# Seven half products instead of eight for the gate matmuls of the last two token chunks, and a written order for the kernel's tail

## The chip, the cores and the metric

The kernel runs on one core of one Trainium2 chip. The metric is the device time of one execution in microseconds (us), lower is better. In the text PE is the matmul engine (TensorE), PEld its weight loads, DVE the VectorE, ACT the ScalarE, POOL the GpSimd and SP the engine whose queue issues the output DMAs. PSUM is the matmul accumulator memory, eight banks of 512 fp32 values per partition.

## The reference

An attention stage feeds a gated feed-forward layer. Only the second is touched by the change.

```python
# 8 batches x 8 heads x 576 positions x 64: pooled (4:1) attention plus banded local attention
attn_out = out_up + out_local
x = attn_out.transpose(0, 2, 1, 3).reshape(4608, 512)
# feed-forward, d_model 512, d_ff 1536
gate = np.maximum(x @ w_gate, 0.0)
val  = x @ w_val
out  = gate * val @ w_out            # 4608 x 512, float32
```

## The kernel before

Heads are worked in 32 pairs. For each pair the kernel loads q, k and v, transposes q and k, computes scores, exponentials and their products with v, and writes the normalised result, transposed, into `xT` (128 partitions x 4 blocks of the model dimension x 4608 tokens, fp16). The feed-forward layer runs over nine chunks of 512 tokens (`TCH`), c = 0 to 8, and over twelve blocks of 128 columns of d_ff, jj = 0 to 11. Attention of later pairs and feed-forward of earlier chunks are interleaved.

The first layer for one chunk and one block (`emit_h_mm`, line 588) is four matmuls of 128x128 by 128x512 with `wg_sb` into one PSUM bank (the gate part) and four with `wv_sb` into the next bank (the value part). ACT then writes `relu` of the gate bank to an fp16 tile (`emit_relu`, L605), and DVE multiplies that by the value bank into `gT` (`emit_gate`, L609). `gT` has two buffers, one for even and one for odd chunks.

The second layer is already done in seven products. A `Unit` (chunk c, half u of 256 tokens) splits the product of `gT` and `wo_sb` into 2 x 2 blocks: 128 tokens, 768 of d_ff, 256 output columns. DVE makes the sums `s1` to `s4` of blocks of `gT` (`sums`, L678); those of the weights, `wt`, were made once. The products `p1` to `p7` are six 256-column matmuls each (`mm`, L684). They accumulate in three PSUM regions `a`, `b` and `d`: ACT copies `a` out after p1, p6 and p7 (`keep`, L718), DVE adds a copy to `d` or `b` (`c11` L721, `c12` L725, `c22` L733), ACT copies the last `a` (`c21` L729), and SP issues the output DMAs (L635).

The order on all engines is written by the kernel: within each engine, instructions run as they were emitted, and the framework only adds the semaphore waits. Chunks 2 to 6 run from a token list (`ORDER`, by `emit_periods`). The tokens with `<` belong to the chunk before: the last two gate multiplications of chunk 6 (`gate/5`, `gate/4`) and the first sums of its second unit (`next/0`, `next/1`) are emitted at the head of the following period.

The rest, the tail, is emitted by loops. `emit_tail_slot` takes three blocks jj of chunks 7 and 8 at a time. It puts one product of a unit of the chunk before between two blocks, and defers each block's relu and gate multiplication until the next block's matmuls have been emitted. Chunk 7 or 8 uses banks 0 to 3 (pairs 0 and 1) for the first layer, and the unit in work uses one bank for each of its regions (4, 5 and 6). At the end the two units of chunk 8 run interleaved, the first in banks 4, 5 and 6, the second in 7, 2 and 3:

```python
        for p in ("p2", "p6", "p5", "p7", "p4", "p3"):
            for x in last:
                x.step(p)
```

POOL has no work after the attention stage: its row is empty in the last 11 of 40 slices of the span.

Of the kernel before, what the change touches and what calls it, by code (L numbers as in the profile page):

```python
# [83 lines left out]
def kernel(  # L84
# [28 lines left out]
    NK = NJJ // 2  # L113
# [5 lines left out]
    keep = ctx.enter_context(tc.tile_pool(name="keep", bufs=1))  # L119
# [22 lines left out]
    qkfull = ring(NL, [128, 2, 2 * NB * 64], FP16, "qk16_")  # L142
# [4 lines left out]
    vwfull = ring(NL, [128, 2 * NB, 128], FP16, "vw_")  # L147
# [14 lines left out]
    gT = ring(2, [128, NJJ, TCH], FP16, "gT_")  # L162
    xT = keep.tile([128, NPB, NTOK], FP16, name="xT")
    ps = psum.tile([128, 8, 512], FP32, name="ps")
# [8 lines left out]
    sa = [  # L173
        [vwfull[r].rearrange("p b c -> p (b c)")[:, 768 * i : 768 * (i + 1)]
         .rearrange("p (j t) -> p j t", t=128) for r in rs for i in range(2)]
        for rs in ((4, 5), (6, 0))
    ]
# [25 lines left out]
    def pair(i):  # L203
        return ps[:, 2 * i : 2 * i + 2, :]
# [377 lines left out]
        else:  # L582
            nc.vector.tensor_copy(out=o, in_=pair(pp)[:, :, 0:288])

    def emit_h_mm(c, jj, pp, which, kks):
        w = (wg_sb, wv_sb)[which]
        for kk in kks:
            nc.tensor.matmul(  # L588
                out=pair(pp)[:, which, :],
                lhsT=w[:, kk, bass.ts(jj, 128)],  # L590
                rhs=xT[:, kk, c * TCH : (c + 1) * TCH],
                start=(kk == 0),
                stop=(kk == 3),
            )

    def emit_h(c, jj, pp, parts=((0, range(4)), (1, range(4))), relu=False):
        for which, kks in parts:
            emit_h_mm(c, jj, pp, which, kks)

        r = emit_relu(pp) if relu else None  # L600
        return lambda: emit_gate(c, jj, pp, emit_relu(pp) if r is None else r)

    def emit_relu(pp):
        r1 = ffn.tile([128, TCH], FP16, name="r1", tag="r1")
        nc.scalar.activation(out=r1, in_=pair(pp)[:, 0, :], func=AF.Relu)  # L605
        return r1

    def emit_gate(c, jj, pp, r1):
        nc.vector.tensor_tensor(  # L609
            out=gT[c % 2][:, jj, :], in0=r1, in1=pair(pp)[:, 1, :], op=ALU.mult  # L610
        )

    def emit_y(c, ty, bank, cut=0, inner=None):
# [39 lines left out]
    units = {}  # L653

    class Unit:


        def __init__(self, c, u, regions, ss, ms, split):
            self.c, self.u, self.split, self.done = c, u, split, []
            self.a, self.b, self.d = (ps[:, k, lo : lo + 256] for k, lo in regions)  # L660
            self.s1, self.s2, self.s3, self.s4 = ss
            self.m1, self.m2, self.m3 = ms
            g = gT[c % 2]
            self.x = [
                [g[:, NK * i : NK * (i + 1), 256 * u + 128 * t : 256 * u + 128 * t + 128] for i in range(2)]
                for t in range(2)
            ]
# [49 lines left out]
        def keep(self, i):  # L717
            nc.scalar.copy(out=(self.m1, self.m2, self.m3)[i], in_=self.a)  # L718
# [29 lines left out]
        def out(self, t, k):  # L748
            if self.split:
                emit_out(self.c, 2 * self.u + t, self.y[t], nc.sync, 256 * k, 256 * k + 256)  # L750
            else:
                self.done.append(t)
                if self.done.count(t) == 2:
                    emit_out(self.c, 2 * self.u + t, self.y[t], nc.sync)
# [51 lines left out]
        emit_s2(hp, 6, 0)  # L806
        emit_warm(1)

    def tail_unit(c, u, banks=(4, 5, 6)):
        return Unit(c, u, [(k, 0) for k in banks], sa[u], sums[u], True)  # L810

    def slot_unit(s):

        c, u = s // 4 - 1, s % 4 // 2
        if s >= NP - LEAD:
            return tail_unit(c, u)
        k = 2 * (((s - PS) // 2 + 1) % 2)
        return Unit(c, u, ((k, 0), (k + 1, 0), (k + 1, 256)), sx, sums[0], False)

    def emit_tail_slot(s, gate):  # L820
        c, jj = s // 4, 3 * (s % 4)
        gate()
        if s % 2 == 0:
            if s == NP - LEAD:
                w = units[s]
                w.sums(5, NK, range(2))
                w.step("p1")
                w.sums(which=range(2, 4))
                emit_h_mm(c, jj, 1, 0, range(3))
                emit_h_mm(c, jj, 1, 1, range(3))  # L830
                w.step("p2")
                emit_h(c, jj, 1, ((0, range(3, 4)), (1, range(3, 4))))()
                emit_h(c, jj + 1, 0)()
            else:
                w = units[s] = slot_unit(s)
                w.sums()
                w.step("p1")
                emit_h(c, jj, 0)()
                w.step("p2")
                emit_h(c, jj + 1, 1)()  # L840
            w.step("p6")
            w.step("p5")
        else:
            w = units[s - 1]
            w.step("p7")
            emit_h(c, jj, 0)()
            w.step("p4")
            if s == 4 * NCH - 1:
                last[0].sums(0, 4)
            emit_h(c, jj + 1, 1)()  # L850
            w.step("p3")
            if s == 4 * NCH - 1:
                last[1].sums(0, 4)
        return emit_h(c, jj + 2, 1 if s == NP - LEAD else 0)

    def unit(c, u):
        s = 4 * (c + 1) + 2 * u
        if s not in units:
            units[s] = slot_unit(s)
        return units[s]  # L860

    relus = {}

    def emit_step(kind, arg, u, c):

        banks = (u, 1 - u)
        i = int(arg[-1]) if arg and arg[-1].isdigit() else 0
        if kind in H_STEPS:
            pp, jj = banks[i % 2], 6 * u + i
            if kind == "relu":  # L870
                relus[c, u, i] = emit_relu(pp)
            elif kind == "gate":
                emit_gate(c, jj, pp, relus.pop((c, u, i)))
            else:
                emit_h_mm(c, jj, pp, int(kind == "hv"), range(4))
        elif kind in UNIT_STEPS:
            UNIT_STEPS[kind](unit(c - 1, u), i)
        elif kind == "next":
# [48 lines left out]
    def emit_periods(c0, c1):  # L927
        for base in range(c0 - 2, c1 + 2):
            for tok in ORDER.split():
                c = base + {">": 1, "<": -1}.get(tok[-1], 0)  # L930
                kind, arg, u = tok.rstrip("<>").split("/")
                if c0 <= c < c1 or c == c0 - 1 and f"{kind}/{arg}/{u}" in LATE:
                    emit_step(kind, arg, int(u), c)

# [71 lines left out]
    with tc.manual_schedule(engines={ET.PE, ET.DVE, ET.Activation, ET.SP, ET.Pool}):  # L1006
        nc.scalar.dma_start(cst_sb[:, 960:1080], cst_dr[:, 960:1080])
        emit_in(0)
        nc.sync.dma_start(cst_sb[:, 0:960], cst_dr[:, 0:960])
        nc.sync.dma_start(cst_sb[:, 1080:1368], cst_dr[:, 1080:1368])  # L1010
        for hp in range(1, 4):
            emit_in(hp)
        emit_warm(10)
        emit_qkT_pe(0, 2, 3)
        emit_pads()
        emit_warm(3)
        for hp in range(LEAD):
            emit_fill(hp)
        gate = None
        for s in range(PS):  # L1020
            gate = emit_slot(s, gate)
        emit_periods(PS // 4, (NP - LEAD) // 4)
        last = [tail_unit(NCH - 1, u, b) for u, b in ((0, (4, 5, 6)), (1, (7, 2, 3)))]
        gate = lambda: None
        for s in range(NP - LEAD, NCH * 4):
            gate = emit_tail_slot(s, gate)
        gate()
        for x in last:
            x.step("p1")
        for which in (range(2), range(2, 4)):  # L1030
            for x in last:
                x.sums(4, NK, which)
        for p in ("p2", "p6", "p5", "p7", "p4", "p3"):
            for x in last:
                x.step(p)


# [28 lines left out]
```

## Time and profile before

| what | before |
|---|---|
| median of 6 runs | 350.24 us (348.64 to 352.86) |
| the profiled execution | 349.6 us |
| its span, first to last instruction | 347.8 us |
| PE busy | 339.5 us (98%) |
| DVE busy | 272.9 us (78%) |
| ACT busy | 214.6 us (62%) |
| POOL busy | 191.0 us (55%) |
| mean granted PE clock | 0.995 of full speed |

The profile's page gives, for each engine, the busy time over the span; then the same in 40 slices; then the DMA queues, the chain of work that ended last, and groups of instructions with the mean duration of one. Further views cut the trace into stretches, or list the instructions of a stretch in order of time. Consecutive instructions of one engine overlap a little, so their starts lie closer together than their durations say; [...]its real pace is read from starts. The tail is the stretch from 274.75 us, where the first product of unit (6, 0) starts, to the end.

### The profile page before, as it was taken

Reading aid. Unit: us, or ns where it says so; the run is one execution under the profiler, and the core shown is the slowest. Engines: PE = TensorE matmul, PEld = TensorE weight load, DVE = VectorE, ACT = ScalarE, POOL = GpSimd, SP = SyncE. Lnnn points to the kernel's source line nnn. Section 1 sums busy time; section 2 is a strip of 40 time slices with the busy share of each in tenths; the row PEclk is TensorE's granted clock in tenths of the full one; section 3 lists DMA queues with packets and bytes.
Section 4 is the critical chain, followed back from the end, with each engine's and each line's share of the span. In section 5 each row is a group of like instructions: output and inputs, shape, how many; then the busy total and the mean of one; then the engine's idle time right before and its main releaser. Section 6 shows DMA issues by size and latency. Waiting matters only on the chain. (4 is left out here: it accounts for less than half of the span.)

```text
span 347.8 us, 7968 instructions
## 1 busy us (share of the span) xinstructions
PE 339.5 (98%) x3127; PEld 205.1 (59%) x3127; DVE 272.9 (78%) x479; ACT 214.6 (62%) x390; POOL 191.0 (55%) x233
## 2 busy tenths in 40 slices
PE   6999999999999999999999999999999999999996
PEld 2665555555565756565666556665666555555575
DVE  4896656788799999999999999999989745354481
ACT  3667777586666776677667767676777443333332
POOL 8985656999999893979398949740300000000000
PEclk9899999999999999999999999999999999999999
DMA  9999999999999999999999998990101001001013
GB/s 144 165 171 186 186 190 164 168 149 192 174 158 147 168 182 83 133 146 188 81 121 166 155 102 103 151 156 10 61 3 60 2 30 47 30 32 45 18 45 121
DMA packets 168772, 40.29 MB, mean 116 GB/s; under 512 B 150080, under 2 KB 165664, under 8 KB 168736
## 3 DMA queue, kind: packets, MB, share of 16 engines
q0 software_dynamic: 132960, 22.93, 88.9%
q1 hardware_dynamic: 35056, 15.79, 24.6%
q10 hardware_dynamic: 720, 1.08, 0.9%
q8 instruction: 24, 0.39, 0.5%
q14 instruction: 12, 0.10, 0.1%
HBM read 46.45 MB, written 9.44 MB: 161 GB/s over the span
## 5 line engine op out<-in xcount | busy, mean ns | idle before, releaser
L588 PE MATMUL ps<-xT,wg_sb 128*128 128x512 f16 x432 | 110.0, 380 | 0.1
L588 PE MATMUL ps<-xT,wv_sb 128*128 128x512 f16 x432 | 109.6, 379 | 0.4 <-DVE gT L609 0.4
L609 DVE TENSOR_TENSOR gT<-r,ps 128x512 f16<-128x512 f16 x108 | 73.0, 682 | 38.1 <-PE ps L588 30.7
L605 ACT ACTIVATE r<-ps 128x512 f16<-128x512 f32 x108 | 64.2, 595 | 49.3 <-PE ps L588 47.6
L588 PEld LDWEIGHTS <-wv_sb 128*128 128x128 f16 x432 | 41.0, 98 | 47.0 <-issue 1.0
L588 PEld LDWEIGHTS <-wg_sb 128*128 128x128 f16 x432 | 39.9, 98 | 36.9 <-DVE xT L581 0.6
L545 DVE TENSOR_TENSOR xn<-ps,rden 64x720 f16<-64x720 f32 x46 | 41.6, 905 | 7.1 <-ACT rden L541 6.2
L376 ACT ACTIVATE ee<-ps 112x576 f16<-112x576 f32 x64 | 38.1, 648 | 10.6 <-PE ps L366 9.5
L536 ACT ACTIVATE rden<-ps 64x720 f32<-64x720 f32 x46 | 35.2, 765 | 14.7 <-PE ps L526 13.7
L233 POOL DMA_DIRECT2D qk<-in_q_dram x46 | 33.7, 735 | 6.9 <-DMA wo_sb<-in_moe_w_out_dram 2.8
L327 POOL TENSOR_TENSOR vd<-v 72x256 f16<-72x256 f32 x23 | 20.4, 896 | 30.6 <-PE ps L526 30.0
L382 DVE TENSOR_TENSOR ee<-ee,cst_sb 112x576 f16<-112x576 f16 x64 | 31.6, 512 | 3.6 <-ACT ee L376 2.6
L684 PEld LDWEIGHTS <-gT 128*128 128x128 f16 x288 | 28.2, 98 | 10.3
L233 POOL DMA_DIRECT2D qk<-in_k_dram x46 | 33.7, 735 | 0.5 <-DMA qk<-in_k_dram 0.4
L258 POOL DMA_DIRECT2D vw<-in_v_dram x30 | 28.7, 957 | 7.5 <-PE ps L294 2.6
L275 DVE TENSOR_REDUCE qkd<-qkT 128x288 f16<-128x1152 f16 x23 | 30.9, 1344 | 0.0
L321 POOL TENSOR_TENSOR v<-v 72x512 f32<-72x512 f16 x23 | 29.0, 1262 | 3.1 <-DMA v<-in_v_dram 2.6
L718 ACT COPY q<-ps 128x256 f32<-128x256 f32 x39 | 14.5, 372 | 20.9 <-PE ps L684 20.7
L684 PEld LDWEIGHTS <-xo 128*128 128x128 f16 x240 | 22.7, 98 | 6.5 <-DVE xo L678 0.8
L684 PE MATMUL ps<-wo_sb,gT 128*128 128x256 f16 x192 | 24.9, 273 | 0.0
L504 DVE TENSOR_TENSOR xT<-xn 128x576 f16<-128x576 f16 x28 | 21.6, 772 | 0.6
L390 ACT ACTIVATE ed<-ps 72x576 f16<-72x576 f32 x32 | 20.6, 643 | 0.0
(103 smaller groups left out, 476.4 us busy)
## 6 DMA issues: line engine op xcount, KB each, us to landing
out_dram<-y_sb SPq DMA_DIRECT2D x20, 256.0 KB, 3.0
vw<-in_v_dram POOLq DMA_DIRECT2D x30, 168.0 KB, 6.8
qk<-in_q_dram POOLq DMA_DIRECT2D x46, 72.0 KB, 6.1
qk<-in_k_dram POOLq DMA_DIRECT2D x46, 72.0 KB, 6.3
v<-in_v_dram POOLq DMA_DIRECT2D x23, 144.0 KB, 6.3
out_dram<-y_sb SPq DMA_DIRECT2D x22, 128.0 KB, 1.7
wg_sb<-in_moe_w_gate_dram POOLq DMA_DIRECT2D x4, 384.0 KB, 9.6
wv_sb<-in_moe_w_val_dram POOLq DMA_DIRECT2D x4, 384.0 KB, 10.8
```

What stands on the lines that cost most here:

```text
L233: nc.gpsimd.dma_start(dst.rearrange("p (j h d) -> p j h d", h=2, d=64)[:, :, hh, :], _dap(src, off + hh * S * D, [[D, 96], [NQ * D, NB], [ ...
L258: nc.gpsimd.dma_start(t, _dap(v, base, [[D, WK], [NQ * D, n], [1, D]]))
L275: nc.vector.tensor_reduce(out=qkd[hp % 2].rearrange("p i t -> p (i t)"), in_=qkT[hp % 4][:, 0 : 2 * S].rearrange("p (t f) -> p t f", f=4), ...
L321: nc.gpsimd.tensor_tensor(out=m, in0=t[:, :, 0:128], in1=t[:, :, 128:256], op=ALU.add)
L376: nc.scalar.activation(out=o, in_=ps[0:WK, p0 + 2 * g : p0 + 2 * g + 2, 0:288], func=AF.Exp, scale=scale)
L382: nc.vector.tensor_tensor(out=o, in0=o, in1=_sap(masks_sb, (0, WK), 288 * g, [[0, 2], [1, 288]]), op=ALU.mult,)
L536: nc.scalar.activation(out=rden[lo : lo + 64], in_=ps[de : de + 64, 4 + 2 * hh : 6 + 2 * hh, 0:360], func=AF.Ln)
L545: nc.vector.tensor_tensor(out=xn[lo : lo + 64], in0=ps[lo : lo + 64, 4 + 2 * hh : 6 + 2 * hh, 0:360], in1=rden[lo : lo + 64], op=ALU.mult,)
L588: nc.tensor.matmul(out=pair(pp)[:, which, :], lhsT=w[:, kk, bass.ts(jj, 128)], rhs=xT[:, kk, c * TCH : (c + 1) * TCH], start=(kk == 0), st ...
L605: nc.scalar.activation(out=r1, in_=pair(pp)[:, 0, :], func=AF.Relu)
L609: nc.vector.tensor_tensor(out=gT[c % 2][:, jj, :], in0=r1, in1=pair(pp)[:, 1, :], op=ALU.mult)
L684: nc.tensor.matmul(out=out, lhsT=left[:, i, :], rhs=right[i], start=(first and i == 0), stop=(i == NK - 1), skip_group_check=True,)
```

## The change

The gate part of chunks 7 and 8 is regrouped into six pairs per chunk of d_ff blocks (j, j + 6), j = 0 to 5. For ten of these twelve pairs (chunk 7 with j = 2 to 5, chunk 8 with j = 0 to 5) the gate part is computed in seven half products; the other two pairs, and the value part of all pairs, stay direct. A pair is a product of 256 columns of d_ff by 512 of the model dimension by 512 tokens, split into 2 x 2 blocks, and a half product `q1` to `q7` is two matmuls of 256 columns.

- DVE makes four sums of the gate weights (`wg`, each 128 x 2 x 768, once) and four sums of `xT` for each of the two chunks (`xs`, each 128 x 2 x 256). They are kept in space that is no longer in use: the q/k tiles and `xT` of chunks 1 and 2.
- A `Block` has three regions in two banks: `a` in bank k, `b` and `d` in the two halves of bank k + 1, with k = 0 for even j and 2 for odd j. ACT copies `a` after q1, q6 and q7 (`keepg`, 128x256 fp32); DVE adds a copy to `d` (`tg/11`), to `b` (`tg/22`, and `tg/12` after q3); ACT copies the last `a` (`tg/21`). The four results lie in SBUF as fp32.
- The relu of these pairs is no longer an ACT instruction: `gateg`, a DVE `scalar_tensor_tensor`, takes max(gate, 0) from SBUF times the value part from PSUM.
- The value part uses bank 4 for block j and bank 5 for block j + 6. The units have regions in two banks, `a` in one, `b` and `d` in the next: banks 6 and 7, and for unit (8, 1) banks 4 and 5.
- The tail is no longer emitted by loops. It comes from a list of tokens, `TAIL`, which interleaves both layers, and which holds the last steps of chunk 6 (`gate/5`, `gate/4`, `next/0`, `next/1`) that the period list had issued. The sums of chunk 8's units are cut in three (`part`, d_ff blocks 0-2, 3-4 and 5) instead of two. The code has steps for half products of the value part too, and for sums on POOL; the list uses neither.

Everything ahead of the tail keeps its instructions and their order.

```diff
+TAIL = """
+p/1/60 wg/2/ hv/0/70 keep/1/60 hg/0/70 gate/5 gate/4 hv/1/70 relu/0/70 sumhi/0/60 next/0 hg/1/70
+sumhi/1/60 next/1 xs/0/7 hg/1/71 relu/1/70 xs/1/7 wg/0/ p/2/60 qg/1/72 gate/0/70 qg/2/72
+keepg/1/72 hg/0/71 relu/1/71 tg/11/72 gate/1/70 p/6/60 sum/2/60 hv/0/71 keep/2/60 wg/1/
+relu/0/71 hv/1/71 xs/2/7 gate/0/71 qg/1/73 qg/6/72 p/7/60 c11//60 keepg/2/72 xs/3/7 keepg/1/73
+qg/7/72 wg/3/ hv/0/72 keepg/3/72 keep/3/60 qg/6/73 qg/5/72 qg/4/72 tg/22/72 p/4/60 gate/1/71
...
+hv/1/80 sum/0/70 p/1/70
+gateg/1/80 qg/6/81 gateg/0/80 p/3/61 keepg/2/81 sum/2/70 qg/7/81 hv/0/81 keepg/3/81 sum/1/70
...
+hv/0/85 part/01/80 part/01/81 part/21/81 p/4/71 part/10/80 part/30/80 c22//71 qg/3/85 c21//71
+hv/1/85 tg/12/85 tg/21/85 gateg/0/85 p/3/71 gateg/1/85 p/1/81 part/22/81 c12//71 p/1/80
+part/21/80 part/11/80 part/31/80 p/2/80 keep/1/80 part/02/80 part/12/80 keep/1/81 p/2/81 c11//80
+part/10/81 p/6/80 part/22/80 part/11/81 part/30/81 p/5/80 part/32/80 keep/2/80 part/02/81
+part/12/81 p/7/80 p/6/81 keep/3/80 c22//80 p/4/80 keep/2/81 part/31/81 c11//81 p/7/81 c21//80
+part/32/81 p/5/81 keep/3/81 p/3/80 c22//81 p/3/81 c12//80 p/4/81 c12//81 c21//81
+"""
...
-    def tail_unit(c, u, banks=(4, 5, 6)):
-        return Unit(c, u, [(k, 0) for k in banks], sa[u], sums[u], True)
+    def tail_unit(c, u):
+        k = 4 if (c, u) == (NCH - 1, 1) else 6
+        return Unit(c, u, ((k, 0), (k + 1, 0), (k + 1, 256)), sa[u], sums[u], True)
...
+        def q(self, i):
+            g, c, j = (wg_sb, wv_sb)[self.w], self.c, self.j
+            x, s = xs[c - NCH + 2], ws[self.w]
+            col = bass.ts(j, 128)
+            out, left, right = (
+                (self.a, g[:, 0:2, col], x_half(c, 0, 0)),
+                (self.d, g[:, 2:4, col], x_half(c, 1, 0)),
+                (self.b, s[3][:, :, col], x_half(c, 1, 1)),
+                (self.a, g[:, 2:4, bass.ts(j + NK, 128)], x[3]),
+                (self.b, s[0][:, :, col], x[0]),
+                (self.a, s[1][:, :, col], x[1]),
+                (self.a, s[2][:, :, col], x[2]),
+            )[i - 1]
+            for k in range(2):
+                nc.tensor.matmul(
...
+        def keep(self, i):
+            nc.scalar.copy(out=self.m[i], in_=self.a)
...
+        elif kind in ("gateg", "gateb"):
+            nc.vector.scalar_tensor_tensor(
+                out=gT[c % 2][:, j + NK * i, :],
+                in0=block(c, j, 0).t[i],
+                scalar=0.0,
+                in1=ps[:, 4 + i, :] if kind == "gateg" else block(c, j, 1).t[i],
+                op0=ALU.max,
+                op1=ALU.mult,
+            )
...
@@ -929,6 +1064,8 @@
+                if c == c1 - 1 and base > c:
+                    continue
...
-        last = [tail_unit(NCH - 1, u, b) for u, b in ((0, (4, 5, 6)), (1, (7, 2, 3)))]
-        gate = lambda: None
-        for s in range(NP - LEAD, NCH * 4):
-            gate = emit_tail_slot(s, gate)
...
+        for tok in TAIL.split():
+            kind, arg, *at = tok.split("/")
+            if at:
+                emit_tail_step(kind, arg, at[0])
+            else:
+                emit_step(kind, arg, 1, NCH - 3)
```

In a token, `hg/0/71` is the direct gate part of block j = 1 of chunk 7 (`hg/1/71` that of block 7), `hv` the value part, `qg/6/72` half product q6 of pair 2 of chunk 7, and `p/7/60` product p7 of unit (6, 0). `part/12/80` is the last third of sum s2 of unit (8, 0).

More of the change, by code (lines that the diff above doesn't have):

```diff
@@ new lines @@
+qg/3/72 c21//60 p/5/60 sum/0/61 tg/21/72 tg/12/72 qg/2/73 hv/1/72 keepg/2/73 tg/11/73 sum/1/61
+qg/7/73 gateg/0/72 p/1/61 keepg/3/73 c22//60 qg/5/73 qg/4/73 gateg/1/72 qg/1/74 tg/21/73 hv/0/73
+tg/22/73 keepg/1/74 xs/0/8 keep/1/61 qg/2/74 sum/3/60 qg/1/75 qg/6/74 tg/11/74 qg/3/73 p/6/61
+tg/12/73 keepg/2/74 qg/5/74 p/3/60 keepg/1/75 qg/2/75 c12//60 qg/7/74 hv/1/73 gateg/0/73
+keepg/3/74 tg/11/75 qg/4/74 p/2/61 tg/22/74 tg/21/74 gateg/1/73 qg/6/75 qg/1/80 qg/3/74
+keepg/1/80 hv/0/74 tg/12/74 keep/2/61 xs/1/8 keepg/2/75 qg/5/75 c11//61 qg/2/80 sum/3/61 qg/7/75
@@ new lines @@
+hv/1/74 keepg/3/75 tg/22/75 qg/4/75 sum/2/61 p/5/61 gateg/0/74 qg/6/80 qg/3/75 gateg/1/74 p/7/61
+tg/12/75 hv/0/75 xs/2/8 keepg/2/80 xs/3/8 tg/21/75 qg/2/81 gateg/0/75 qg/7/80 hv/1/75 keepg/3/80
+tg/11/80 keep/3/61 qg/1/81 p/4/61 keepg/1/81 tg/11/81 qg/4/80 c21//61 qg/5/80 c22//61 hv/0/80
+tg/21/80 tg/22/80 gateg/1/75 qg/1/82 qg/3/80 keepg/1/82 qg/5/81 tg/12/80 hv/1/80 sum/0/70 p/1/70
+gateg/1/80 qg/6/81 gateg/0/80 p/3/61 keepg/2/81 sum/2/70 qg/7/81 hv/0/81 keepg/3/81 sum/1/70
+keep/1/70 c12//61 qg/2/82 tg/22/81 qg/4/81 hv/1/81 tg/11/82 qg/3/81 qg/6/82 tg/12/81 p/2/70
@@ new lines @@
+sum/3/70 keepg/2/82 p/6/70 tg/21/81 gateg/0/81 qg/7/82 sum/0/71 keep/2/70 qg/5/82 qg/2/83
+keepg/3/82 p/7/70 tg/22/82 qg/4/82 keep/3/70 qg/1/83 qg/3/82 keepg/1/83 p/4/70 tg/12/82
+gateg/1/81 hv/0/82 c21//70 c11//70 qg/6/83 tg/11/83 p/5/70 keepg/2/83 sum/2/71 tg/21/82 p/1/71
+gateg/0/82 qg/7/83 c22//70 keep/1/71 qg/1/84 qg/2/84 keepg/3/83 qg/5/83 hv/0/83 keepg/1/84
+tg/22/83 qg/3/83 qg/6/84 tg/12/83 qg/4/83 p/3/70 tg/11/84 tg/21/83 gateg/0/83 keepg/2/84 hv/1/82
+sum/1/71 qg/7/84 gateg/1/82 qg/1/85 keepg/3/84 p/6/71 keepg/1/85 c12//70 qg/5/84 part/20/80
@@ new lines @@
+qg/2/85 tg/22/84 hv/1/83 part/00/80 sum/3/71 qg/3/84 qg/4/84 tg/12/84 hv/0/84 tg/21/84
+gateg/1/83 p/2/71 tg/11/85 qg/6/85 c11//71 hv/1/84 keepg/2/85 gateg/0/84 keep/2/71 qg/5/85
+gateg/1/84 qg/7/85 p/5/71 keepg/3/85 p/7/71 part/00/81 tg/22/85 qg/4/85 part/20/81 keep/3/71
+hv/0/85 part/01/80 part/01/81 part/21/81 p/4/71 part/10/80 part/30/80 c22//71 qg/3/85 c21//71
+hv/1/85 tg/12/85 tg/21/85 gateg/0/85 p/3/71 gateg/1/85 p/1/81 part/22/81 c12//71 p/1/80
+part/21/80 part/11/80 part/31/80 p/2/80 keep/1/80 part/02/80 part/12/80 keep/1/81 p/2/81 c11//80
@@ L583, in emit_x_pe, with emit_h_mm @@
             nc.vector.tensor_copy(out=o, in_=pair(pp)[:, :, 0:288])
-    def emit_h_mm(c, jj, pp, which, kks):
+    def emit_h_mm(c, jj, pp, which, kks, out=None):
         w = (wg_sb, wv_sb)[which]
@@ L588, in emit_h_mm @@
             nc.tensor.matmul(
-                out=pair(pp)[:, which, :],
+                out=pair(pp)[:, which, :] if out is None else out,
                 lhsT=w[:, kk, bass.ts(jj, 128)],
@@ L601, in emit_h, with emit_relu, emit_gate @@
         return lambda: emit_gate(c, jj, pp, emit_relu(pp) if r is None else r)
-    def emit_relu(pp):
+    def emit_relu(pp, h1=None):
         r1 = ffn.tile([128, TCH], FP16, name="r1", tag="r1")
-        nc.scalar.activation(out=r1, in_=pair(pp)[:, 0, :], func=AF.Relu)
+        nc.scalar.activation(out=r1, in_=pair(pp)[:, 0, :] if h1 is None else h1, func=AF.Relu)
         return r1
-    def emit_gate(c, jj, pp, r1):
+    def emit_gate(c, jj, pp, r1, h2=None):
         nc.vector.tensor_tensor(
-            out=gT[c % 2][:, jj, :], in0=r1, in1=pair(pp)[:, 1, :], op=ALU.mult
+            out=gT[c % 2][:, jj, :], in0=r1, in1=pair(pp)[:, 1, :] if h2 is None else h2, op=ALU.mult
         )
@@ L818, in slot_unit @@
         return Unit(c, u, ((k, 0), (k + 1, 0), (k + 1, 256)), sx, sums[0], False)
[L820 to L854, printed above, removed]
     def unit(c, u):
@@ L860, in unit @@
         return units[s]
+    ws = [
+        qkfull[0:4],
+        [vwfull[3].rearrange("p b c -> p (b c)").rearrange("p (i c) -> p i c", i=2)] + qkfull[4:7],
+    ]
+    xs = [
+        [xT[:, i, lo : lo + TCH].rearrange("p (k t) -> p k t", k=2) for i in range(4)]
+        for lo in (TCH, 2 * TCH)
+    ]
+    ht = [
+        [
+            [xT[:, 2 * w + m, 2 * TCH * k + TCH : 2 * TCH * k + 3 * TCH].bitcast(FP32) for m in range(2)]
+            for k in (1, 2)
+        ]
+        for w in range(2)
+    ]
@@ new lines, with emit_ws @@
+    hm = [
+        [vwfull[r].rearrange("p b c -> p (b c)")[:, TCH * i : TCH * (i + 1)].bitcast(FP32) for i in range(3)]
+        for r in (1, 2)
+    ]
+    def emit_ws(w, i, lo, hi, eng):
+        g = (wg_sb, wv_sb)[w]
+        a11, a12, a21, a22 = (
+            g[:, 2 * k : 2 * k + 2, 768 * m + lo : 768 * m + hi] for m in range(2) for k in range(2)
+        )
+        s1, s2, s3, s4 = (t[:, :, lo:hi] for t in ws[w])
+        o, a, b, op = (
+            (s1, a21, a22, ALU.add),
+            (s2, s1, a11, ALU.subtract),
+            (s3, a11, a21, ALU.subtract),
+            (s4, a12, s2, ALU.subtract),
+        )[i]
+        eng.tensor_tensor(out=o, in0=a, in1=b, op=op)
@@ new lines, in x_half, with emit_xs, __init__, out @@
+    def x_half(c, k, n):
+        return xT[:, 2 * k : 2 * k + 2, c * TCH + 256 * n : c * TCH + 256 * n + 256]
+    def emit_xs(c, i):
+        (b11, b12), (b21, b22) = [[x_half(c, k, n) for n in range(2)] for k in range(2)]
+        t1, t2, t3, t4 = xs[c - NCH + 2]
+        o, a, b = ((t1, b12, b11), (t2, b22, t1), (t3, b22, b12), (t4, b21, t2))[i]
+        nc.vector.tensor_tensor(out=o, in0=a, in1=b, op=ALU.subtract)
+    class Block:
+        def __init__(self, c, j, w, k):
+            self.c, self.j, self.w = c, j, w
+            self.a, self.b, self.d = (ps[:, b, lo : lo + 256] for b, lo in ((k, 0), (k + 1, 0), (k + 1, 256)))
+            self.t = ht[w][j % 2]
+            self.m = hm[w]
+        def q(self, i):
[13 more added lines that the diff above has]
+                nc.tensor.matmul(
+                    out=out,
+                    lhsT=left[:, k, :],
+                    rhs=right[:, k, :],
+                    start=(k == 0 and i in (1, 2, 5)),
+                    stop=(k == 1),
+                    skip_group_check=True,
+                )
+        def keep(self, i):
+            nc.scalar.copy(out=self.m[i], in_=self.a)
+        def out(self, arg):
+            lo = {"11": 0, "12": 256, "21": 0, "22": 256}[arg]
+            o = self.t[arg[0] == "2"][:, lo : lo + 256]
+            if arg == "21":
+                nc.scalar.copy(out=o, in_=self.a)
+                return
+            src, m = {"11": (self.d, 0), "12": (self.b, 1), "22": (self.b, 2)}[arg]
+            nc.vector.tensor_tensor(out=o, in0=src, in1=self.m[m], op=ALU.add)
@@ new lines, with block, emit_tail_step @@
+    held = keep.tile([128, 1], FP16, name="held")
+    blocks = {}
+    def block(c, j, w):
+        if (c, j, w) not in blocks:
+            blocks[c, j, w] = Block(c, j, w, 4 if w else 2 * (j % 2))
+        return blocks[c, j, w]
+    def emit_tail_step(kind, arg, at):
+        c, j = (int(at[0]), int(at[1])) if len(at) == 2 else (int(at or 0), 0)
+        i = int(arg[0]) if arg else 0
+        if kind in ("hg", "hv"):
+            w = int(kind == "hv")
+            bank = 4 + i if w else 2 * (j % 2) + i
+            emit_h_mm(c, j + NK * i, None, w, range(4), ps[:, bank, :])
+        elif kind == "relu":
+            relus[c, j, i] = emit_relu(None, ps[:, 2 * (j % 2) + i, :])
+        elif kind == "gate":
+            emit_gate(c, j + NK * i, None, relus.pop((c, j, i)), ps[:, 4 + i, :])
+        elif kind in ("gateg", "gateb"):
[6 more added lines that the diff above has]
+                op1=ALU.mult,
+            )
+        elif kind == "xs":
+            emit_xs(c, i)
+        elif kind == "wg":
+            emit_ws(0, i, 0, 768, nc.vector)
+        elif kind == "hold":
+            nc.gpsimd.tensor_tensor(out=held, in0=ws[0][3][:, 0, 0:1], in1=xs[0][3][:, 0, 0:1], op=ALU.add)
+        elif kind == "wv":
+            emit_ws(1, i, 192 * int(arg[1]), 192 * int(arg[1]) + 192, nc.gpsimd)
+        elif kind in ("qg", "qv"):
+            block(c, j, int(kind == "qv")).q(i)
+        elif kind in ("keepg", "keepv"):
+            block(c, j, int(kind == "keepv")).keep(i - 1)
+        elif kind in ("tg", "tv"):
+            block(c, j, int(kind == "tv")).out(arg)
+        elif kind == "part":
+            lo, hi = ((0, 3), (3, 5), (5, 6))[int(arg[1])]
+            unit(c, j).sums(lo, hi, (i,))
+        else:
+            UNIT_STEPS[kind](unit(c, j), i)
@@ L1022 @@
         emit_periods(PS // 4, (NP - LEAD) // 4)
-        last = [tail_unit(NCH - 1, u, b) for u, b in ((0, (4, 5, 6)), (1, (7, 2, 3)))]
-        gate = lambda: None
-        for s in range(NP - LEAD, NCH * 4):
-            gate = emit_tail_slot(s, gate)
[L1027 to L1035, printed above, removed]
+        for tok in TAIL.split():
+            kind, arg, *at = tok.split("/")
+            if at:
+                emit_tail_step(kind, arg, at[0])
+            else:
+                emit_step(kind, arg, 1, NCH - 3)
 _INS = ['q', 'k', 'v', 'moe_w_gate', 'moe_w_val', 'moe_w_out']
```

## The prediction

> **What bounds the kernel now.** I read the page first, then the chain that ended last, then the tail in stretches, and last its instructions in order of time.
>
> ```profile
> PE 339.5 (98%) x3127; PEld 205.1 (59%) x3127; DVE 272.9 (78%) x479; ACT 214.6 (62%) x390; POOL 191.0 (55%) x233
> ...
> PE 20%; DVE 0%; issue 0%
> PE ps L588 12%; PE ps L684 8%; DVE gT L609 0%; DVE y_sb L725 0%
> ```
>
> The chain is PE work from 276 us to the end:
>
> ```profile
> 276.01 0.61 DVE gT L609
> 276.62 0.04 issue
> 276.66 0.81 PE ps L588 x3
> ...
> 283.97 1.73 PE ps L588 x8
> 285.70 0.66 PE ps L684 x6
> ...
> 335.30 9.21 PE ps L684 x84
> 344.50 0.02 issue
> 344.52 0.42 DVE y_sb L725
> ```
>
> Eight 512-column matmuls take 1.73 us (0.216 each), six 256-column ones 0.655 (0.109). Only one wait stands in it, at the top: 276.66 follows the three matmuls begun at 275.40, which end at 276.05, so a gate multiplication holds PE for 0.61 us. The stretches show the room beside PE:
>
> ```profile
> 294.75:304.75 10.00, 10.00 (x63) 5.97 (x61) 3.51 (x6) 3.33 (x8) 0.00 (x0) 1.00 0.11 39
> 304.75:314.75 10.00, 10.00 (x63) 5.97 (x61) 5.48 (x10) 3.34 (x7) 0.00 (x0) 1.00 0.08 28
> 335.13:344.32 9.19, 9.19 (x85) 8.11 (x83) 4.80 (x16) 2.98 (x8) 0.00 (x0) 1.00 0.20 71
> ```
>
> After the stretch come PE, PEld, DVE, ACT and POOL busy, then the clock. PE is full at clock 1.00, DVE at a third to a half. So matmul time taken out of the tail comes off the span, if the other engines deliver in time.
>
> **The change, part by part.** Times without a row count from the first matmul of p/1/60, at 274.75.
>
> *PE.* The tail now is 24 blocks x 1.727 + 252 unit matmuls x 0.1092 + 0.61 = 69.58 us; the trace has 344.32 - 274.75 = 69.57. A direct pair's gate part is 8 x 0.2159 = 1.727, seven half products are 14 x 0.1092 = 1.529: 0.198 saved, x10 = 1.98 us. All else on PE keeps its count. That a group of two keeps the pace that L684's groups of six have is an assumption (weight loads take 98 ns beside 109).
>
> *The wait at the top.* hg/1/70, which needs the bank that `gate/5` frees, now comes at 3.25 (p 0.66 + hv, hg, hv 0.86 each). DVE ends the last xT sum at 0.54, then wg/2 0.95, gate/5 0.69: free at 2.2; gate/4 at 2.8, needed at 4.11. The 0.61 goes. Late next would be qg/6/72 at 9.53: it needs wg/1, and DVE works without a break from 0.54 until that is done, at about 8.8.
>
> *DVE.* Added: 4 wg of 1536 elements. Rows of this kind (L678) give 0.22 for 128 and 0.55 for 768, so 0.95 on their line; the nearest unpaired row (L504, 576 in 0.77) would make it 1.75. I take 0.95; at 1.75 three of them make qg/6/72 about 1.7 late, once. 8 xs at 0.42 = 3.4; 30 tg like L721/L725/L733 at 0.42 = 12.6; finer cuts of the last sums, 24 for 16 pieces, +1.2. `gateg` has no row. Nearest is the product it replaces, 512 elements from PSUM at 0.69; below, 0.42 (the fp16 sum of 512); above, a second pass of 512 at L545's 1.04 ns, 1.22. I take 0.69: twenty for twenty, nothing (at 1.22, +10.6). Sum 3.8 + 3.4 + 12.6 + 1.2 = 21.0 on 37.3, in 47 more instructions. Successive ones start before the last ends:
>
> ```profile
> 338.01 0.42 DVE L721 TENSOR_TENSOR y_sb<-ps,q 128x256 f32<-128x256 f32 x1
> 338.35 0.41 DVE L721 TENSOR_TENSOR y_sb<-ps,v 128x256 f32<-128x256 f32 x1
> ```
>
> 0.34 apart for 0.42: 0.08 overlap, so 37.3 + 21.0 - 47 x 0.08 = 54.5 of 67.0 us. The Trainium skill, "VectorE: DVE Perf Modes", section "The DRAIN you can't avoid", says that the next operation doesn't start until the pipe is empty, though one that is not held may start earlier. By the strict rule all 128 instructions add up to 61.3, 91% of the tail, before any wait. The row decides, and I use 54.5.
>
> *ACT.* 40 copies of 0.37 for 20 relus of 0.60: +2.9 on 23.3, 26.2 of 67. Its load hides; its latency doesn't:
>
> ```profile
> 280.12 0.82 PE L684 MATMUL ps<-wt,vw 128*128 128x256 f16 x6
> 280.97 0.37 ACT L718 COPY q<-ps 128x256 f32<-128x256 f32 x1 [0.92 <-PE ps L684]
> ```
>
> The six take until 280.78, ACT starts 0.20 later; with 0.37 and 0.04 to the waiting matmul (276.62 to 276.66) a keep's round trip is 0.61. Between qg/6/72 and qg/7/72 the list puts one p, 0.655: margin 0.04. The same margin stands at qg/7/81, p/7/70, p/4/70, p/7/80, p/4/80, p/7/81.
>
> *Added DVE waits.* hv/0/81 (34.32) waits for gateg/0/80, queued behind gateg/1/80, which waits for hv/1/80 (ends 32.57): 32.57 + 0.22 + 0.61 + 0.69 + 0.04 = 34.13, margin 0.19. Behind it on PE stands everything else. At the end, qg/3/85 ends at 56.29; + 0.22 + tg/12/85 0.42 + 0.04 + gateg/0/85 0.69 + 0.04 = 57.70 for p/1/81 at 57.81. p/3/81 at 65.67 needs c22//81, which needs p/5/81 (ends 65.01): + 0.22 + 0.42 + 0.04 = 65.69, late by 0.02.
>
> *Two regions in one bank.* The skill, "PSUM — Partial Sum Buffer", section "PSUM bank collisions raise a hardware error", says to guard by bank, not by address. The built instruction list does so: p/5/70 (region b) waits for c11//70 (region d). That speaks against the change, since the old tail gave each region its own bank. The tightest such place, laid out with the rows above, is p/5/70 at 41.94, with 0.10 in hand: by the rule 0 to 0.1 lost, by addresses 0. I take 0.
>
> *Other queues.* SP and POOL keep their instructions in order; output DMAs still come in pairs 0.65 apart or more. The last is fed by an ACT copy (0.37) instead of a DVE sum (0.42): -0.05.
>
> *Sum.* -1.98 - 0.61 - 0.05 = -2.64. For the seven keep places, p/3/81 and the like, eight at 0.05: +0.4. Net -2.24: PE's tail 67.4, span 345.6, and 349.6 - 2.24 = 347.4 for the profiled execution. The median of the runs is 0.64 above it: 350.24 - 2.24 = 348.0.
>
> **The rivals.**
>
> *DVE falls behind (same).* If `gateg` costs about 1.0, or operations don't overlap while they wait for three engines, DVE is near full between 8 and 35, where wg, xs and five blocks fall together: by their places in the list, 35 instructions of 18.0 us start between 10 and 30. Without overlap each 10 us stretch lacks 1.4 us of its cover, and single waits reach 1 to 1.5 us around qg/5/74 and again at p/6/81, where the sums of unit (8, 1) come last. They are not additive, since a late PE gives DVE time. For it: the narrow margins. Against: 338.35 above. I put the loss at 1.5 to 2: -0.9, 349.3.
>
> *A group of two breaks the weight prefetch (slower).* Seventy half products each have their own wait and other weights. If the 98 ns load of the first weights is not hidden behind the matmul in front, each loses up to 0.098: 6.9 us, -2.64 + 6.9 = +4.3, 354.5. It decides from 0.038 a group (2.64 / 70), and makes it slower by over 0.5% from 0.063. Against: the switch from L588 to L684 at 285.54 costs nothing, and attention runs groups of three and two, some with waits of their own, at an unbroken pace:
>
> ```profile
> 269.64 0.29 PE L518 MATMUL ps<-ee,vw 112*128 112x96 f16 x3
> 269.77 0.23 PE L526 MATMUL ps<-ed,vd 72*128 72x72 f16 x2
> 269.84 0.29 PE L518 MATMUL ps<-ee,vw 112*128 112x96 f16 x3
> ```
>
> *It saves nothing.* If 256-column groups ran at 0.123 a matmul, seven half products would cost as much as eight; L684's 0.109 excludes it for long groups, and for short ones it is the rival above.
>
> **How the numbers follow.** The sum as laid out: 0.67. DVE behind, or several small losses: 0.22. Slower: 0.11. A measurement of this kernel can tell about 0.5%, 1.75 us. The likeliest case, -1.8 to -2.6, lies beyond that, so faster takes 0.67, within 0.5% 0.22, slower 0.11. Low: all waits hidden, 350.24 - 2.64 = 347.6, less 0.7 for how far a set of runs can lie from another (this median stands 0.64 from the profiled execution): 346.9. High: past the DVE case to a small loss, 350.8; the rest of the slower case is left out.
>
> **What would show it.** Right: L684 and the new matmul line both pace at 0.109; PE's tail 67.4 us from its first product; no wait of PE on DVE at the top; waits of PE on the copies and sums under 1 us in all; DVE 50 to 58 us busy after 275; `gateg` at 0.69. Wrong: PE waiting for the new DVE lines by 1 us or more in the first half of the tail (DVE case), idle before weight loads put down to issue or a pace over 0.13 in the half products (prefetch), or a final chain running through DVE sums instead of PE.

## The result, and the profile after

| what | before | changed |
|---|---|---|
| median of the runs beside each other | 350.51 us (40 runs) | 347.67 us (19 runs) |
| ratio | | 0.9917, 95% interval 0.9900 to 0.9934 |
| span of the profiled execution | 347.8 us | 345.1 us |
| tail, first product of unit (6, 0) to the last matmul's end | 69.57 us | 67.06 us |

The change makes the kernel faster by 2.9 us (350.51 x 0.0083), with an interval of 2.3 to 3.5. The forecast was 348.0 from a gain of 2.24.

The page of the changed kernel shows PE with less work and DVE with more:

```profile
PE 337.2 (98%) x3187; PEld 210.8 (61%) x3187; DVE 290.7 (84%) x529; ACT 215.3 (62%) x410; POOL 190.2 (55%) x233
```

The stretches of the tail, with the same columns as in the prediction, the first from 274.75 and then one in the middle and the last:

```profile
274.75:284.75 10.00, 10.00 (x62) 5.91 (x61) 9.53 (x20) 3.54 (x8) 0.00 (x0) 1.00 0.00 0
304.75:314.75 10.00, 10.00 (x78) 7.44 (x77) 7.73 (x17) 3.48 (x12) 0.00 (x0) 1.00 0.12 40
332.50:342.00 9.50, 9.29 (x85) 7.98 (x82) 5.98 (x23) 2.68 (x8) 0.00 (x0) 1.00 0.36 115
```

PE stays full at clock 1.00 while DVE goes from about half of the tail (37.3 of 69.57 us) to four fifths (54.1 of 67.06), and in the first stretch to 95%. Matmuls in order of time at the head of the tail (start, length, line, form, count):

```profile
274.57 0.82 PE L718 MATMUL ps<-wo_sb,gT 128*128 128x256 f16 x6
275.23 1.03 PE L622 MATMUL ps<-xT,wv_sb 128*128 128x512 f16 x4
276.09 1.03 PE L622 MATMUL ps<-xT,wg_sb 128*128 128x512 f16 x4
276.96 1.03 PE L622 MATMUL ps<-xT,wv_sb 128*128 128x512 f16 x4
277.82 1.89 PE L622 MATMUL ps<-xT,wg_sb 128*128 128x512 f16 x8
279.55 0.82 PE L718 MATMUL ps<-wo_sb,gT 128*128 128x256 f16 x6
280.20 0.60 PE L928 MATMUL ps<-xT,wg_sb 128*128 128x256 f16 x4
280.64 1.03 PE L622 MATMUL ps<-xT,wg_sb 128*128 128x512 f16 x4
...
284.10 0.38 PE L928 MATMUL ps<-xT,qk 128*128 128x256 f16 x2
284.32 0.82 PE L718 MATMUL ps<-wt,vw 128*128 128x256 f16 x6
```

Every start follows the one before at the pace of its matmuls: 0.86 for four of 512 columns, 0.66 for six of 256, and for the half products (L928) 0.44 for four and 0.22 for two. The wait of 0.61 us at the top is gone: the eight gate matmuls at 277.82 (hg/1/70 and hg/1/71) find their banks free. From here to the end the starts leave one gap, within the twelve matmuls of the first of these two lines:

```profile
339.59 1.55 PE L718 MATMUL ps<-wo_sb,vw 128*128 128x256 f16 x12
340.97 0.82 PE L718 MATMUL ps<-wt,gT 128*128 128x256 f16 x6
```

Twelve at 0.109 are 1.31, and the next start comes 1.38 later: p/3/81, the second six of the twelve, waits for the DVE sum `c22` of the same unit and loses 0.07 us. The groups of the new DVE and ACT work between 275 and 346 us (count, busy us, mean ns):

```profile
L969 DVE SCALAR_TENSOR_TENSOR gT<-xT,ps 128x512 f16<-128x512 f32 x20 | 13.4, 681 | 0.7 <-PE ps L622 0.3
L947 DVE TENSOR_TENSOR xT<-ps,vw 128x256 f32<-128x256 f32 x30 | 12.4, 422 | 7.4 <-PE ps L928 3.2 <-ACT vw L938 2.9 <-ACT q L752 0.9
L938 ACT COPY vw<-ps 128x256 f32<-128x256 f32 x30 | 10.8, 374 | 20.7 <-PE ps L928 13.8 <-DVE xT L947 6.8
L903 DVE TENSOR_TENSOR xT<-xT 128x512 f16<-128x512 f16 x8 | 3.3, 419 | 0.1
L894 DVE TENSOR_TENSOR qk<-wg_sb 128x1536 f16<-128x1536 f16 x2 | 1.9, 952 | 0.0
```

`gateg` takes 0.681 us, the sums of weights 0.952, the others 0.42 and 0.37.

### The profile page after: what moved, and what is told of

It reads as the page before. It is cut to its first block, busy times and chain, and to the rows that moved or that the text cites. A ratio compares the mean times of both kernels' runs of the same rounds, so it can differ in the third digit from the quotient of the medians.

```text
span 345.1 us, 8159 instructions
## 1 busy us (share of the span) xinstructions
PE 337.2 (98%) x3187; PEld 210.8 (61%) x3187; DVE 290.7 (84%) x529; ACT 215.3 (62%) x410; POOL 190.2 (55%) x233
## 4 chain that ended last, share of the span: by engine, by line
PE 91%; DVE 3%; DMA 2%; ACT 1%; issue 1%; ACTq 0%; POOLq 0%
PE ps L622 48%; PE ps L718 20%; PE ps L928 4%; PE ps L552 3%; PE ps L652 3%; PE ps L400 2%; PE ps L389 2%; PE ps L328 2%; PE ps L560 2%; DMA qk<-in_k_dram 2%; PE ps L825 1%; DVE xo L474 1%; PE ps L373 1%; DVE xo L712 1%; PE ps L486 1%
## 5 line engine op out<-in xcount | busy, mean ns | idle before, releaser
L622 PE MATMUL ps<-xT,wg_sb 128*128 128x512 f16 x352 | 89.1, 380 | 0.1
L643 DVE TENSOR_TENSOR gT<-r,ps 128x512 f16<-128x512 f16 x88 | 59.2, 681 | 11.9 <-ACT r L639 6.3
L639 ACT ACTIVATE r<-ps 128x512 f16<-128x512 f32 x88 | 52.3, 595 | 26.4 <-PE ps L622 26.2
L622 PEld LDWEIGHTS <-wg_sb 128*128 128x128 f16 x352 | 32.0, 98 | 32.3 <-DVE xT L615 0.6
L579 DVE TENSOR_TENSOR xn<-ps,rden 64x720 f16<-64x720 f32 x46 | 41.7, 906 | 6.2 <-ACT rden L575 5.0
L416 DVE TENSOR_TENSOR ee<-ee,cst_sb 112x576 f16<-112x576 f16 x64 | 31.2, 508 | 3.5 <-ACT ee L410 2.7
L938 ACT COPY vw<-ps 128x256 f32<-128x256 f32 x30 | 10.8, 374 | 20.7 <-PE ps L928 13.8
L538 DVE TENSOR_TENSOR xT<-xn 128x576 f16<-128x576 f16 x28 | 22.9, 817 | 0.6
```

The source lines that it names most:

```text
L416: nc.vector.tensor_tensor(out=o, in0=o, in1=_sap(masks_sb, (0, WK), 288 * g, [[0, 2], [1, 288]]), op=ALU.mult,)
L579: nc.vector.tensor_tensor(out=xn[lo : lo + 64], in0=ps[lo : lo + 64, 4 + 2 * hh : 6 + 2 * hh, 0:360], in1=rden[lo : lo + 64], op=ALU.mult,)
L622: nc.tensor.matmul(out=pair(pp)[:, which, :] if out is None else out, lhsT=w[:, kk, bass.ts(jj, 128)], rhs=xT[:, kk, c * TCH : (c + 1) * TCH],
L639: nc.scalar.activation(out=r1, in_=pair(pp)[:, 0, :] if h1 is None else h1, func=AF.Relu)
L643: nc.vector.tensor_tensor(out=gT[c % 2][:, jj, :], in0=r1, in1=pair(pp)[:, 1, :] if h2 is None else h2, op=ALU.mult)
```

## The experiments

The spans of the profiled executions can't be set against each other to a tenth: the tail's first product started between 274.2 and 277.1 us in the kernels below whose instructions ahead of it are the same. So the measure is the length of the tail, from the first start of p/1/60 to the start of the last group plus its matmuls at 0.109. The ratio to the kernel before stands beside it.

### The written list with direct gate parts, and with four pairs

Each pair's seven half products become two direct blocks, with relu and `gate`, at places where their banks are free; sums that are no longer needed go. An excerpt:

```diff
...
-qg/7/72 wg/3/ hv/0/72 keepg/3/72 keep/3/60 qg/6/73 qg/5/72 qg/4/72 tg/22/72 p/4/60 gate/1/71
-qg/3/72 c21//60 p/5/60 sum/0/61 tg/21/72 tg/12/72 qg/2/73 hv/1/72 keepg/2/73 tg/11/73 sum/1/61
+hg/1/72 relu/1/72 p/4/60 gate/1/71 hg/0/72 relu/0/72 c21//60 p/5/60 sum/0/61 hv/1/72 sum/1/61
...
```

> The written tail list, but with the gate part of all twelve pairs direct: no half products, no sums of weights or xT. PE work from the tail's first product is 24 blocks x 1.727 + 252 x 0.1092 = 68.97 us. If the gain is the half products' 1.98 us plus the 0.61 us wait at the top (my theory), this keeps only the second: tail 69.0 us, span about 347.2, ratio to the kernel before 0.998. If it was the written order of the tail that earned the time (rival), it stays near the changed kernel: tail 67.1 us, ratio 0.992. If the list is worse than the loops for direct blocks, tail over 69.6, ratio above 1.000.

Tail 69.20 us, 0.23 of it waits in three places; ratio 0.9992 (0.9969 to 1.0015). In this version and in the first one with four pairs, relus of some pairs overwrote those of the pair two before, so that some blocks were multiplied with another pair's relu: the same amount of work on other values. With four pairs:

> The written list with half products in chunk 7 alone, four pairs, and chunk 8 direct. My theory, 0.198 us a pair: 68.97 - 4 x 0.198 = 68.2 us of tail, ratio 0.996, between the list without half products and the changed kernel. A fixed cost of the scheme (sums of weights at the head of the tail) would show as less than that: 68.5 to 69.0. The rival of the written order: 67.1 us.

Tail 68.34, 0.17 of it waits; ratio 0.9981 (0.9962 to 1.0001). Both again, with four tiles in turn for the relus instead of two:

```diff
-            relus[c, j, i] = emit_relu(None, ps[:, 2 * (j % 2) + i, :])
+            r1 = xT[:, 2 + i, TCH * ((j + 2 * c) % 4 + 3) : TCH * ((j + 2 * c) % 4 + 4)]
+            nc.scalar.activation(out=r1, in_=ps[:, 2 * (j % 2) + i, :], func=AF.Relu)
+            relus[c, j, i] = r1
```

> The written list with all gate parts direct again, each relu now with a tile of its own (in the first version the relu of pair j + 2 shared a tile with pair j). Same arithmetic as there: 68.97 us of PE work, tail 69.0 to 69.3, ratio 0.998. If the shared tiles had held the first version up by a hidden wait, the tail falls under 68.97, which my theory excludes, since PE's work alone takes that long.

> Half products in chunk 7 alone, relus of chunk 8 in tiles of their own. Theory of 0.198 us a pair: 68.97 - 0.79 = 68.18, and 0.1 to 0.2 of waits: tail 68.2 to 68.4. A fixed cost of the scheme: over 68.5.

Tails 69.10 (0.13 waits) and 68.27 (0.07 waits); ratios 0.9985 (0.9962 to 1.0009) and 0.9972 (0.9943 to 1.0001). The two tails as one stretch each, without pairs and with four (the stretch, then PE, PEld, DVE, ACT and POOL busy, and the clock):

```profile
275.87:344.97 69.10, 69.10 (x445) 43.34 (x443) 37.40 (x87) 22.38 (x47) 0.00 (x0) 1.00 0.12 41
276.52:344.79 68.27, 68.27 (x469) 45.68 (x467) 46.40 (x107) 22.89 (x55) 0.00 (x0) 1.00 0.13 41
```

Less the waits, PE's work is 68.97 with no pair, 68.20 with four and 66.99 with ten: 0.19 a pair for the first four, 0.20 for the other six, 0.198 over all. With the waits left in, the tails of 69.10, 68.27 and 67.06 give 0.21 and 0.20. The written order by itself takes away the wait at the top and gives no more; the rest of the gain is proportional to the pairs, and a fixed cost of the scheme on PE is not seen, to a few hundredths of a microsecond.

### The kernel before, with two gate multiplications swapped

```diff
+            if base == c1:
+                i, j = toks.index("gate/5/1<"), toks.index("gate/4/1<")
+                toks[i], toks[j] = toks[j], toks[i]
```

> The kernel before, with one swap: at the head of the tail gate/4 (frees bank pair 1, which the next block uses) stands ahead of gate/5. My theory: the only wait of PE in the tail, 0.61 us from start to start, goes, since gate/4 then ends about 0.6 earlier; tail 69.57 - 0.61 = 68.96 us, span about 347.2, ratio 0.998. Rival: the wait only moves to the block in pair 0 that comes next, and the tail stays at 69.5.

Tail 68.98 us; ratio 0.9988 (0.9968 to 1.0008). In order of time, first the kernel before, then with the swap:

```profile
275.40 0.81 PE L588 MATMUL ps<-xT,wg_sb 128*128 128x512 f16 x3
276.66 0.81 PE L588 MATMUL ps<-xT,wv_sb 128*128 128x512 f16 x3 [0.45 <-DVE gT L609]
```

```profile
275.73 0.81 PE L588 MATMUL ps<-xT,wg_sb 128*128 128x512 f16 x3
276.39 0.81 PE L588 MATMUL ps<-xT,wv_sb 128*128 128x512 f16 x3
277.03 0.82 PE L684 MATMUL ps<-wo_sb,gT 128*128 128x256 f16 x6
```

The value part now starts 0.66 after the gate part, three matmuls later, where before it started 1.26 later (275.40 to 276.66). One swapped pair of instructions takes 0.59 us off the tail, and no other wait of the old tail is longer than 0.03 us. That part of the gain did not need the half products. By time alone it is too small to tell: the interval spans 1.

### More work on DVE

```diff
             )
+            for _ in range(1):
+                nc.vector.tensor_tensor(
+                    out=vwfull[2].rearrange("p b c -> p (b c)")[:, 0:512],
+                    in0=wg_sb[:, 0, 0:512], in1=wg_sb[:, 1, 0:512], op=ALU.add,
+                )
```

> The changed kernel with one DVE sum more behind each gateg (128x512 fp16, 0.42 us long, 0.34 from start to start, result never used): 20 x 0.34 = 6.8 us more on DVE, 53.9 + 6.8 = 60.7 of 67 us. If the tail's narrow margins count (0.04 to 0.35 us at a dozen places), PE waits 0.5 to 2 us: tail 67.6 to 69.1, ratio 0.994 to 0.998. If DVE's 13 idle us are real slack: tail 67.1 to 67.3, ratio 0.992. If DVE is the bound already: over 70, ratio above 1.000.

Tail 68.37 us, with 1.36 of waits in seven places, the longest 0.31; DVE 59.7 us busy in it; ratio 0.9983 (0.9960 to 1.0007). That is the outcome expected if the narrow margins count. With two of them:

> The changed kernel with two unused DVE sums behind each gateg: 13.6 us more on DVE, 53.9 + 13.6 = 67.5 us, as much as PE has. One such sum cost 1.31 us of tail (68.37 - 67.06). If DVE is the bound from here on (margin theory), the tail is DVE's work plus what it must wait at both ends, about 0.5 at the head and 3.5 at the end: 70 to 72 us, slower than the kernel before, ratio 1.002 to 1.007. If losses only grow in proportion: 67.06 + 2.6 = 69.7, ratio 1.000.

Tail 75.67 us with 8.7 of waits; ratio 1.0162 (1.0117 to 1.0208): slower than expected by either theory. The tail as one stretch in the changed kernel, with one and with two sums more:

```profile
274.57:341.63 67.06, 67.06 (x505) 49.20 (x503) 54.08 (x129) 23.61 (x67) 0.00 (x0) 1.00 0.13 42
```

```profile
275.39:343.76 68.37, 68.00 (x505) 49.09 (x503) 59.70 (x149) 23.61 (x67) 0.00 (x0) 1.00 0.13 41
```

```profile
277.08:352.75 75.67, 69.70 (x505) 49.03 (x503) 67.82 (x169) 23.50 (x67) 0.00 (x0) 1.00 0.11 37
```

Four of PE's seven rows of waits in the last one, with total, times and longest:

```profile
PE ps L928 <- DVE xT L947: 2.1, 5, 0.9
PE ps L718 <- DVE y_sb L759: 1.2, 1, 1.2
PE ps L622 <- DVE gT L969: 0.8, 1, 0.8
...
PE ps L718 <- DVE y_sb L755: 0.5, 1, 0.5
```

The first 5.6 us of extra DVE time cost 1.3, the next 8.1 cost 7.3. DVE is not simply full in the last case either: it stands still for 75.67 - 67.82 = 7.85 us. Of these, 2.2 are waits of `c22` for ACT's copies at the very end, where the changed kernel has 2.3; for most of the others, too, the trace names products of PE or ACT's copies of them. That PE and DVE hold each other up in turn is my reading of it. So 5.6 us more of DVE work take half of the tail's gain (1.31 of 2.51), and 13.7 us make the kernel slower than before. Where below 5.6 the gain begins to melt was not measured, and the extra work was tried only behind each `gateg`.

### A longer round trip over ACT

```diff
             nc.scalar.copy(out=self.m[i], in_=self.a)
+            nc.scalar.copy(out=hm[1][0], in_=self.a)
```

> The changed kernel with a second, unused copy of region a behind each keepg, which the next half product must wait for as well: 30 x about 0.28 us on ACT (24 of 67 us busy before, 32 with it), and 0.28 us more in each round trip from a half product over ACT to the next one in the same bank. Theory of latency (margins of 0.03 at qg/7/72 and qg/7/81 and of 0.20 to 0.25 at qg/4/73, qg/7/75, qg/4/74, qg/4/75): those come late by 0.03 to 0.25 each, 0.7 in all, less what one wait saves the next: tail 67.4 to 67.9. Theory of load (ACT has 43 idle us): nothing, 67.0 to 67.1.

Tail 67.92 us, ratio 0.9928 (0.9892 to 0.9964). ACT is busy for 31.7 us of 67, so more than half of its time is free, yet the tail grows by 0.86. The gaps between PE's starts stand where the margins were thin: 0.24 at qg/7/72, 0.20 at qg/7/75, 0.23 at qg/7/81, 0.03 to 0.09 at four others. At the first of them, the six matmuls of p/7/60 take 0.66, and qg/7/72 starts 0.90 behind their start:

```profile
283.98 0.82 PE L718 MATMUL ps<-wt,vw 128*128 128x256 f16 x6
284.88 0.38 PE L928 MATMUL ps<-xT,qk 128*128 128x256 f16 x2
```

What counts on ACT here is the delay of one copy, not its load.

### The sums of weights on POOL

```diff
-            emit_ws(0, i, 0, 768, nc.vector)
+            emit_ws(0, i, 0, 768, nc.gpsimd)
```

> The changed kernel with the four sums of gate weights on POOL instead of DVE. DVE loses 4 x 0.87 = 3.5 us at the head of the tail. My theory: nothing in PE's tail waited for them, so 67.0 to 67.1 as in the changed kernel and ratio 0.992. Rival: POOL is slow on them (its sums of 512 elements take 1.26 us, so some 3.5 us each, 14 in all from about 262 us on) or disturbs DVE, and qg/6/72 or qg/7/72 waits: tail 67.5 to 69.

Ratio 1.0204 (1.0163 to 1.0244), slower by 7 us, which neither expectation had. The tail is untouched: it runs from 283.66 to 350.72, 67.06 us, as long as in the changed kernel. But it begins 9.1 us later. POOL starts the sums at 246.16, as soon as its own work is done, and they last until 259.2:

```profile
246.16 6.15 POOL L894 TENSOR_TENSOR qk<-wg_sb 128x1536 f16<-128x1536 f16 x2
252.38 3.48 POOL L894 TENSOR_TENSOR qk<-qk,wg_sb 128x1536 f16<-128x1536 f16 x1
255.94 3.28 POOL L894 TENSOR_TENSOR qk<-wg_sb,qk 128x1536 f16<-128x1536 f16 x1
```

DVE at that time, in the changed kernel and in this one:

```profile
249.24 0.74 DVE L538 TENSOR_TENSOR xT<-xn 128x576 f16<-128x576 f16 x1
249.91 0.54 DVE L712 TENSOR_TENSOR xo<-gT 128x768 f16<-128x768 f16 x1
250.60 0.46 DVE L416 TENSOR_TENSOR ee<-ee,cst_sb 112x576 f16<-112x576 f16 x1 [0.16 <-ACT ee L410]
```

```profile
248.62 4.30 DVE L538 TENSOR_TENSOR xT<-xn 128x576 f16<-128x576 f16 x1
252.84 3.43 DVE L712 TENSOR_TENSOR xo<-gT 128x768 f16<-128x768 f16 x1
256.20 3.33 DVE L416 TENSOR_TENSOR ee<-ee,cst_sb 112x576 f16<-112x576 f16 x1
```

The same three instructions take 4.30, 3.43 and 3.33 us. Behind the third, PE waits for 7.5 us for the masked exponentials of L416, and the granted clock falls to 0.83 between 246 and 262 us. I took it that a DVE instruction was held until the running POOL instruction ended, and cut the sums into sixteen:

```diff
-            emit_ws(0, i, 0, 768, nc.vector)
+            for n in range(4):
+                emit_ws(0, i, 192 * n, 192 * n + 192, nc.gpsimd)
```

> The gate weight sums on POOL again, in sixteen pieces of 384 elements instead of four of 1536. With four, three DVE instructions with two SBUF inputs took 4.30, 3.43 and 3.33 us instead of 0.74, 0.54 and 0.46, each ending shortly behind the end of a POOL sum of 3.1 to 3.5. If such a DVE instruction is held until the running POOL instruction ends, no single one takes over about 1.5 us now, more of them are lengthened, and PE is held less: start of the tail 1 to 5 us later than in the changed kernel (274.6) instead of 9, ratio 0.995 to 1.008. If POOL holds DVE for as long as it has work in its queue, the delay stays at 8 to 9 us, ratio 1.02.

Ratio 1.0251 (1.0198 to 1.0303). My theory fell. POOL and DVE:

```profile
245.78 6.99 POOL L894 TENSOR_TENSOR qk<-wg_sb 128x384 f16<-128x384 f16 x8
252.72 3.51 POOL L894 TENSOR_TENSOR qk<-qk,wg_sb 128x384 f16<-128x384 f16 x4
256.18 3.51 POOL L894 TENSOR_TENSOR qk<-wg_sb,qk 128x384 f16<-128x384 f16 x4
```

```profile
248.24 12.07 DVE L538 TENSOR_TENSOR xT<-xn 128x576 f16<-128x576 f16 x1
260.24 0.55 DVE L712 TENSOR_TENSOR xo<-gT 128x768 f16<-128x768 f16 x1
```

One instruction took 12.07 us. It started at 248.24, when POOL was at about the third of its sixteen sums, and ended at 260.31, 0.6 us behind the last one (259.7). The sixteen follow each other without a gap. With four sums, POOL pauses for 0.07 us at 252.31, before the third sum, which reads an earlier result, and for 0.08 at 255.86. The first two lengthened DVE instructions end 0.61 and 0.41 us behind the start of these pauses, and the third 0.31 behind the end of the last sum. So both runs fit the other expectation: DVE is held until POOL pauses, and not only until the running sum ends.

## Why the prediction was right, and where its sizes were off

- *PE's work.* The saving of 0.198 us a pair is what the series of no, four and ten pairs shows (0.19 for the first four, 0.20 for the other six). Half products in groups of two keep the pace of 0.109 that was assumed from groups of six.
- *The wait at the top.* 0.61 forecast, 0.59 when the swap alone takes it away, and no wait left there in the changed kernel. It is not a merit of the half products.
- *The waits that I added.* This is the term that was mis-sized: +0.4 us for eight thin margins. The trace shows 0.07 in all, and all of it at p/3/81 (0.02 forecast). Its path was as forecast, only two of its hops were longer by some hundredths. The margins of 0.04 at the keep round trips were true ones: with about 0.28 us more in the trip, qg/7/72 and qg/7/81 come late by 0.24 and 0.23. I charged seven such margins as if 0.05 were lost at each; in the profiled execution none of them is late. Without that term, and without the 0.05 that I put behind the tail, the sum is -2.59; with the measured wait of 0.07 it is -2.52, and the trace gives 67.06 - 69.57 = -2.51 for the tail. The medians' 2.9 us lies beyond both, but its interval begins at 2.3. The profiled spans differ by 2.7; the 0.2 more than the tail comes ahead of it, where the instructions are the same.
- *DVE.* Forecast 54.5 us busy in the tail, measured 54.1. `gateg` was taken at 0.69 and takes 0.681, the sums of weights at 0.95 and take 0.952. So both prices that I took held, and for the sums of weights the paired rate, not the slower row of L504, was the right neighbour. DVE did not work quite without a break until wg/1 was done, as I had laid out: it stood still for 0.40 us before the sum at 281.03. But wg/1 ended at 8.8 all the same.
- *The end.* Forecast -0.05. From the last matmul's end to the end of the span it is 3.5 us in both kernels (347.8 - 344.32 and 345.1 - 341.63); spans given to a tenth can't tell 0.05 from nothing.
- *The DVE rival* named a real danger that was not reached. With 5.6 us more on DVE, the tail's gain falls to 69.57 - 68.37 = 1.20, near the 0.9 that the rival left of it. The first wait then stands at qg/5/74, as it said, but the longest (0.31) at p/2/80 instead of p/6/81. hv/0/81, whose margin I had put at 0.19, is late by 0.20. A `gateg` of 1.0, which I named as its price, would be 6.4 us more on DVE, near the first of these loads.
- *The prefetch rival* is excluded: two matmuls with their own weights and often a wait take 0.22 us wherever they stand, so the loss per group is under the rounding, against the 0.038 from which it would have decided.
- *The shared bank* (c11//70 before p/5/70) cost nothing in the changed kernel: no gap there, as the rows said. But the wait is real and thin. With one load on DVE p/5/70 is late by 0.21 us, and with two PE waits 0.5 us for `c11` (the row of L755 above), which reads the other region of the same bank.

## What to carry to other kernels

Where one engine bounds a stage to 98%, work taken off it comes back in full as long as the others deliver, and that is decided by the tightest wait in each queue's order, not by the share of busy time: ACT at a third of its time was about four hundredths of a microsecond from costing something. To see how much an engine can still take, add work of known length to it: here 5.6 us on DVE took half of the tail's gain, and 13.7 us more than all of it. And separate what a rewritten order removes from what the arithmetic saves: about a quarter of this gain (0.6 of 2.5 us) was one pair of instructions in the wrong order.

## What the hardware showed that I had not expected

A DVE instruction with two inputs in SBUF was held for as long as POOL had sums queued without a gap: one of 0.74 us took 12.07. Instructions with one input in PSUM ran at their usual length beside the same sums: the two of L579 that start at 246.54 in the run with four sums took 1.82 us together, as in the changed kernel. The Trainium skill, "GPSIMD Engine Reference", section "8. Key points", names the contention for the SBUF interfaces, for DVE instructions with two SBUF inputs among others; these runs agree and add its size, and that cutting POOL's work into smaller instructions did not help (ratio 1.0251 against 1.0204, with intervals that overlap). That the pause came in the attention stage, almost 30 us ahead of where DVE had made the sums (275.0), follows from POOL being idle: it began as soon as its inputs were there. Holding the sums back until the tail was not tried.
